# A retention layer followed by a low-rank mixer and an MLP: program order on all engines, batch pairs as nine chunks, q and k transposed by DMA, row tiles and column tiles on the tensor engine

## The chip, the cores and the metric

The kernel runs on one core of one Trainium2 chip. The metric is the device time of the program in microseconds (us), as the median of several runs. Engines: PE is the tensor engine (matmul), PEld its weight loads, DVE the vector engine, ACT the scalar engine, POOL the GpSimd engine, SP an engine that does nothing but issue DMAs in these kernels.

## The reference

There are 8 batches of 576 tokens, 8 heads of 64 dimensions, a mixer of rank 32 over the tokens, and an MLP 512 -> 2048 -> 512. Inputs and outputs are float32; the kernel computes in bfloat16.

```python
scores = (q @ k.T) / 8                       # per batch and head, 576 x 576
D[i, j] = gamma_h ** (i - j) if i >= j else 0
x = (scores * D) @ v                         # heads side by side: 576 x 512 per batch
h = (x.T @ U @ V).T                          # mixes tokens: U is 576 x 32, V is 32 x 576
u = x + h
out = u + relu(u @ w_ch1) @ w_ch2
```

The kernel does not form the 576 x 576 scores. It works in chunks of 128 tokens. The decay is put into factors of the rows of q and v. Within a chunk it computes scores, masks them ("ret") and multiplies by v; what the earlier chunks of the batch give comes from a running state S = sum of k^T v, by q x S.

## The kernel before

576 is four chunks of 128 and one of 64, so a pair of batches is ten chunks, two of them half empty. Each chunk is loaded as float32 from the SP queue, cast on DVE and scaled on POOL, transposed on PE, and evicted (copied out of PSUM, the memory that matmuls write) on ACT. A 64-row matmul stands in the trace as 64*128, a full one as 128*128, and two of them, one for each half of the rows, start together (120.630 and 120.634 us in the trace of the kernel before, the next two 0.067 later):

```python
def T(c):                                    # 8 transposes of q and k on PE, one eviction on ACT
    for j in range(2):
        for hp in range(NHP):
            nc.tensor.transpose(pst[:, j*NHP+hp, :], t[:, j, 2*hp:2*hp+2, :]..., ident)
    nc.scalar.activation(out=qkT, in_=pst, func=AF.Copy)
def SC(c):                                   # scores: 64-row matmuls, one per head; then the mask on DVE
    nc.tensor.matmul(psc[:, hl, hp, 0:n], qkT[pb:pb+HALF, NHP+hp, :], qkT[pb:pb+HALF, hp, cols], ...)
    nc.vector.tensor_tensor(out=rv[...], in0=psc[...], in1=tri[...], op=ALU.mult)
def RV(c):                                   # ret x v, then q x state over all 128 rows
    nc.tensor.matmul(po[:, h*D:(h+1)*D], ret[:, h, :], t[:, 2, h, :], ...)
    nc.tensor.matmul(po[:, hp*P:(hp+1)*P], qkT[:, hp, :], s_sb[:, hp, :], ...)
    ...
for s in range(NC + 2):                      # order of one batch's attention
    if s < NC:          add(T, s, 460)
    if 0 <= s - 2:      add(RV, s - 2, 450)
    if s < NC - 1:      add(ST, s, 220)
    if 0 <= s - 1 < NC: add(SC, s - 1, 450)
```

`q x state` needs the state without its off-diagonal head blocks, so DVE multiplies it by a block mask. `U^T x` is one 128 x 512 matmul per chunk, with U padded from 32 to 128 columns. The attention and mixer of batch b+1 are interleaved with the MLP of batch b; only PE is in program order, and the scheduler orders the other engines:

```python
with tc.manual_schedule(engines={PE}):
    interleave([], front_items(0))
    for b in range(B):
        if b + 2 < B:
            load_batch(b + 2)
        fill = front_items(b + 1) if b + 1 < B else []
        interleave(mlp_items(b, us[b], pairs[b // 2]), fill)
```

Below, "Y1" is the first MLP product (with the relu on ACT as its eviction), "Y2" the second, and "a pair" is two batches, 1152 tokens.

## Time and profile before

| | before |
|---|---|
| time, median | 395.88 us |
| first Y1 starts | 52.84 us |
| one pair in the steady state (first Y1 of batch 2 to that of batch 4) | 87.3 us |
| from the start of the last matmul to the end | 4.3 us |

The page of the kernel before: busy time of the engines (with the share of the span), then busy tenths of PE, the granted clock of PE and the DMA share in 40 equal slices of the span.

```profile
PE 348.4 (88%) x2784; PEld 200.0 (51%) x2784; DVE 183.1 (46%) x249; ACT 156.2 (40%) x279; POOL 64.2 (16%) x83
...
PE   1244489999999999899999999899999999999996
...
PEclk9999959999999999999999999999999999999999
DMA  8999999726995599485149500011001100010012
```

PE is nearly full from the sixth slice on. No other engine is near full there; DMA is, in some slices up to the 22nd. Before the sixth slice DMA is full and PE is not. The busy time by stretch shows the steady state of the kernel before: batch 2's MLP (with batch 3's attention), then batch 3's. Columns: stretch in us and its length, then busy us and number of instructions of each engine, granted clock, DMA share, GB/s.

```profile
core 0: us, PE busy (x) PEld busy (x) DVE busy (x) ACT busy (x) POOL busy (x), PEclk, DMA share, GB/s
141.32:182.00 40.68, 38.73 (x311) 20.35 (x311) 24.14 (x29) 16.84 (x26) 7.29 (x7) 1.00 0.90 182
182.00:228.58 46.58, 45.40 (x388) 27.90 (x386) 25.14 (x30) 21.46 (x43) 5.21 (x5) 1.00 0.47 109
```

PE is idle for 3 us of these 87. The waits of PE in the kernel before, from 95 to 356 us (total us, times, longest; the second line stands there three times, once per pair):

```profile
PE po L270 <- DVE ret L257: 5.8, 9, 1.1
PE ps_y_1610 L390 <- ACT uT_1496 L354: 0.7, 1, 0.7
```

The instructions of PE in order of time show where that wait stands. Columns: start, duration, engine, line, operation, output and inputs, shapes, count, and in brackets the idle time ahead and what ended it. Durations of matmuls overlap, so what a group costs is read from the distance between starts.

```profile
120.63 0.40 PE L246 MATMUL psc<-qkT 64*128 64x128 bf16 x8
120.96 1.04 PE L401 MATMUL ps_y_1358<-w_sb,y_1027 128*128 128x512 bf16 x4
122.35 0.41 PE L270 MATMUL po<-qkv,ret 128*128 128x64 bf16 x8 [0.35 <-DVE ret L257]
122.59 0.39 PE L277 MATMUL po<-s_sb,qkT 128*128 128x128 bf16 x4
```

Scores cost 0.33 us of PE (120.63 to 120.96), q x state 0.23 (from 122.59 to the next MLP matmul at 122.82). Ahead of the scores stands a gap of 0.1 us: they start 0.31 us after the last full matmul, where full ones of 512 columns follow each other at 0.216. Behind them stands another of 0.09: the last two of the eight start at 120.81, the pairs are 0.056 apart, and the next full matmul comes at 120.96. The texts call these gaps a switch. Only one group of MLP matmuls stands between the scores and `ret x v`; the mask takes 1221 ns on DVE, so PE waits. The eight transposes of a chunk cost 0.45 us (61.17 to 61.62):

```profile
61.17 0.61 PE L207 MATMUL pst<-ident,qkv 128*128 128x128 bf16 x8
61.62 1.03 PE L390 MATMUL ps_y_638<-uT_474,w_sb 128*128 128x512 bf16 x4
```

### The profile page before, as it was taken

Reading aid. Unit: us, or ns where it says so; the run is one execution under the profiler, and the core shown is the slowest. Engines: PE = TensorE matmul, PEld = TensorE weight load, DVE = VectorE, ACT = ScalarE, POOL = GpSimd, SP = SyncE. Lnnn points to the kernel's source line nnn. Section 1 sums busy time; section 2 is a strip of 40 time slices with the busy share of each in tenths; the row PEclk is TensorE's granted clock in tenths of the full one; section 3 lists DMA queues with packets and bytes.
Section 4 is the critical chain, followed back from the end, with each engine's and each line's share of the span. In section 5 each row is a group of like instructions: output and inputs, shape, how many; then the busy total and the mean of one; then the engine's idle time right before and its main releaser. Section 6 shows DMA issues by size and latency. Waiting matters only on the chain. (4 is left out here: it accounts for less than half of the span.)

```text
span 394.6 us, 6659 instructions
## 1 busy us (share of the span) xinstructions
PE 348.4 (88%) x2784; PEld 200.0 (51%) x2784; DVE 183.1 (46%) x249; ACT 156.2 (40%) x279; POOL 64.2 (16%) x83
## 2 busy tenths in 40 slices
PE   1244489999999999899999999899999999999996
PEld 0233245446774455446764455346764455456642
DVE  4436326655456555753557445743334533540021
ACT  2121147305770156216760266117750276027700
POOL 6486123301321212210122002200000000000000
PEclk9999959999999999999999999999999999999999
DMA  8999999726995599485149500011001100010012
GB/s 157 217 184 197 198 224 212 131 69 166 223 209 124 150 207 213 98 196 139 25 97 207 140 28 1 28 42 40 2 2 55 55 27 2 28 53 27 2 53 81
DMA packets 123471, 42.49 MB, mean 108 GB/s; under 512 B 114705, under 2 KB 118833, under 8 KB 123441
## 3 DMA queue, kind: packets, MB, share of 16 engines
q1 hardware_dynamic: 117696, 37.76, 43.4%
q0 software_dynamic: 5744, 4.31, 7.2%
q8 instruction: 22, 0.36, 0.4%
q14 instruction: 9, 0.07, 0.1%
HBM read 36.92 MB, written 9.44 MB: 117 GB/s over the span
## 5 line engine op out<-in xcount | busy, mean ns | idle before, releaser
L390 PEld LDWEIGHTS <-w_sb 128*128 128x128 bf16 x768 | 70.4, 98 | 39.1 <-issue 4.7
L185 POOL TENSOR_TENSOR qkv<-stage_t,vscale 128x512 bf16<-128x512 f32 x32 | 34.7, 1085 | 128.3 <-DMA stage_t<-in_v_dram 65.3
L257 DVE TENSOR_TENSOR ret<-psc,tri 128x1024 bf16<-128x1024 f32 x32 | 39.1, 1221 | 9.3 <-PE psc L246 9.1
L328 ACT ACTIVATE a_sb<-psa 128x512 bf16<-128x512 f32 x8 | 4.8, 597 | 97.2 <-PE psa L322 97.2
L184 DVE CAST qkv<-stage_t 128x1024 bf16<-128x1024 f32 x32 | 30.9, 966 | 24.2 <-PE po L270 12.1
L232 DVE TENSOR_TENSOR s_sb<-pss,bdm 128x512 bf16<-128x512 f32 x32 | 22.1, 689 | 41.5 <-PE pss L225 41.5
L216 ACT ACTIVATE qkT<-pst 128x1024 bf16<-128x1024 bf16 x32 | 32.8, 1024 | 20.1 <-PE pst L207 19.1
L287 DVE TENSOR_TENSOR xt<-po,qscale 128x512 bf16<-128x512 f32 x32 | 22.0, 688 | 33.3 <-PE po L277 25.0
L207 PE MATMUL pst<-ident,qkv 128*128 128x128 bf16 x256 | 21.3, 231 | 15.4 <-DVE qkv L184 14.7
L207 PEld LDWEIGHTS <-qkv 128*128 128x128 bf16 x256 | 18.1, 104 | 22.1 <-DVE qkv L184 15.5
L344 DVE TENSOR_TENSOR ut<-ph,xt 128x512 bf16<-128x512 f32 x32 | 22.0, 690 | 11.9 <-PE ph L335 11.7
L270 PE MATMUL po<-qkv,ret 128*128 128x64 bf16 x256 | 13.7, 200 | 8.2 <-DVE ret L257 8.2
L270 PEld LDWEIGHTS <-ret 128*128 128x128 bf16 x256 | 11.6, 102 | 16.9 <-DVE ret L257 13.8
L225 PE MATMUL pss<-qkv 128*128 128x128 bf16 x112 | 11.6, 231 | 6.7 <-POOL qkv L185 6.7
L351 PE MATMUL pu<-ident,ut 128*128 128x128 bf16 x128 | 13.0, 227 | 4.3 <-DVE ut L344 3.8
L351 PEld LDWEIGHTS <-ut 128*128 128x128 bf16 x128 | 10.0, 101 | 12.7 <-DVE ut L344 5.2
L335 PE MATMUL ph<-a_sb,Vbig 128*128 128x512 bf16 x40 | 14.8, 392 | 0.7 <-ACT a_sb L328 0.7
L225 PEld LDWEIGHTS <-qkv 128*128 128x128 bf16 x112 | 9.2, 103 | 11.1 <-issue 6.8
L246 PE MATMUL psc<-qkT 64*128 64x128 bf16 x256 | 13.6, 229 | 0.0
L246 PEld LDWEIGHTS <-qkT 64*128 64x128 bf16 x256 | 7.7, 98 | 11.2 <-issue 11.2
L401 PEld LDWEIGHTS <-y_4127 128*128 128x128 bf16 x80 | 7.8, 98 | 9.3
L277 PE MATMUL po<-s_sb,qkT 128*128 128x128 bf16 x112 | 11.5, 229 | 0.0
(541 smaller groups left out, 615.7 us busy)
## 6 DMA issues: line engine op xcount, KB each, us to landing
out_dram<-o_sb SPq DMA_DIRECT2D x36, 256.0 KB, 2.1
stage_t<-in_k_dram SPq DMA_DIRECT2D x32, 256.0 KB, 4.8
stage_t<-in_q_dram SPq DMA_DIRECT2D x32, 256.0 KB, 4.9
stage_t<-in_v_dram SPq DMA_DIRECT2D x32, 256.0 KB, 5.0
w_sb<-in_moe_w_ch_dram POOLq DMA_DIRECT2D x16, 128.0 KB, 6.7
w_sb<-in_moe_w_ch_dram POOLq DMA_DIRECT2D x8, 256.0 KB, 10.0
stage_t<-in_k_dram SPq DMA_DIRECT2D x8, 128.0 KB, 3.8
stage_t<-in_q_dram SPq DMA_DIRECT2D x8, 128.0 KB, 3.8
```

The costliest lines, as they stand in the source:

```text
L184: nc.vector.tensor_copy(out=t[rows, 0:2, :, :], in_=f[rows, 0:2, :, :])
L185: nc.gpsimd.tensor_tensor(out=t[rows, 2, :, :], in0=f[rows, 2, :, :], in1=vscale[rows, c, :, None].to_broadcast([L, H, D]), op=ALU.mult,)
L207: nc.tensor.transpose(pst[:, j * NHP + hp, :], t[:, j, 2 * hp:2 * hp + 2, :].rearrange("p h d -> p (h d)"), ident,)
L216: nc.scalar.activation(out=qkT, in_=pst, func=AF.Copy)
L232: nc.vector.tensor_tensor(out=s_sb, in0=pss, in1=bdm[:, None, :].to_broadcast([P, NHP, P]), op=ALU.mult,)
L246: nc.tensor.matmul(psc[:, hl, hp, 0:n], qkT[pb:pb + HALF, NHP + hp, :], qkT[pb:pb + HALF, hp, cols], start=True, stop=True,)
L257: nc.vector.tensor_tensor(out=rv[:, :, :, cols], in0=psc[:, :, :, 0:n], in1=tri[:, None, None, cols].to_broadcast([P, 2, NHP, n]), op=ALU. ...
L270: nc.tensor.matmul(po[:, h * D:(h + 1) * D], ret[:, h, :], t[:, 2, h, :], start=(h == 0), stop=True, skip_group_check=True,)
L287: nc.vector.tensor_tensor(out=xt[rows, :].rearrange("p (h d) -> p h d", d=D), in0=po[rows, :].rearrange("p (h d) -> p h d", d=D), in1=qsca ...
L344: nc.vector.tensor_tensor(out=ut[rows, :], in0=ph[rows, :], in1=x_tiles[c][rows, :], op=ALU.add)
L351: nc.tensor.transpose(pu[:, cc, :], u_tiles[c][:, cc * P:(cc + 1) * P], ident)
L390: nc.tensor.matmul(ps[:, 0:n], w1_sb[:, cc, f * P:(f + 1) * P], uT[:, cc, t0:t0 + n], start=(cc == 0), stop=(cc == NCC - 1),)
```

## The change

Its intent: less work on PE, no waits on PE in the steady state, and an earlier first Y1. It has seven parts.

1. All engines run in program order, so the program's own interleaving decides what each engine does next.
2. A pair of batches is nine chunks; the middle one holds the end of one batch and the start of the next, with a mask of its own.
3. q and k are transposed by DMA in pairs 1 to 3 (27 chunks). Pair 0 keeps PE, as the data come late there.
4. q x state is eight 64-row matmuls right behind the scores, which are 64-row matmuls already. Each head uses its own rows, so the state needs no block mask, and ACT copies it.
5. U^T x is five matmuls of 32 columns each, the first four written to four different groups of 32 rows of pa. V is loaded four times to sum the four parts.
6. Scores and mask are one work item, `ret x v` the next, with MLP work in between. Items are spread evenly over the MLP.
7. At the start k and q are loaded ahead of v, and the weights in pieces between. Outputs are issued from POOL, not SP.

```diff
-    with tc.manual_schedule(engines={PE}):
+    with tc.manual_schedule():
 ...
+    def xbar(pr, i):
+        nc.sync.dma_start_transpose(out=c["qkT"], in_=c["qk"].rearrange("p j n -> p (j n)"))
 ...
+        def A(i):
+            SC(pr, i)
+            if i not in (0, J):
+                QS(pr, i)
+            mask(pr, i)
+        def Bf(i):
+            RV(pr, i)
+            if i == J:
+                QS(pr, i)
+            XS(pr, i)
+            if i not in (J, NI - 1):
+                ST(pr, i)
+                Scopy(pr, i)
 ...
+    def QS(pr, i):                            # row tiles: each head's 64 rows
+                r = slice(hl * HALF, (hl + 1) * HALF)
+                nc.tensor.matmul(c["po"][m, hl, hp * D:(hp + 1) * D],
+                    c["qkT"][r, hp, m], s_sb[r, hp, hl * D:(hl + 1) * D], ...)
 ...
+        def MA():                             # column tiles: 32 columns each
+            for n, i in enumerate(idx):
+                g = slice((n % 4) * R, (n % 4 + 1) * R)
+                nc.tensor.matmul(pa[g, :], Ub[:, n, :], st["x", pr][:, i, :],
+                    start=(n < 4), stop=True, skip_group_check=True)
 ...
-                nc.sync.dma_start(out=out_flat[...], in_=o_sb)
+                nc.gpsimd.dma_start(out=out_flat[r0:r0 + P, :], in_=o_sb)
 ...
+        for i in range(J + 1, NI):            # after the first batch's mixer, before its first Y1
+            cast_qk(0, i, "act")
+            scale_v(0, i)
+        for f in range(0, NF, 2):
+            load_w2(f)
+        merge(y1_items(0), attn_items(0, 1, T=True) + mixer_items(0, 1), aux_items(NI, NI + 5))
```

## The prediction

> **What bounds the kernel now.** The tensor engine (PE), after a slow start. The instructions in order of time show the first MLP matmul at 52.8 us, the last at 390.7; the busy-time table shows PE about 97% busy between, at full clock except from 40 to 60 us (0.87, then 0.62). DVE (46%), ACT (40%) and POOL (16%) have room. DMA is saturated only to about 65 us (768 KB of q, k, v per 3.8 us).
>
> Two batches take 87.2 us (first MLP matmul of batch 2, 141.3 us, to that of batch 6, 315.85, halved). Their MLP is 9 chunks of 6.86 us (last batch, alone: 34.3 us for five): 61.7 us. PE work of attention and mixer, from distances between starts: q/k transposes 10 x 0.445, scores 4.1, ret x v 2.35, q x state 1.8, state 1.8, U^T x 10 x 0.216, V 2.2, u transposes 2.0; together 20.8 us. The other 4.7 us are waits and switches; the waits view names ret x v waiting for the mask (1221 ns on DVE), 1.9 us in each even batch, and the first Y1 behind uT, 0.7.
>
> **Steady state, per pair of batches.**
> - q/k transposes leave PE in pairs 1 to 3: -4.45 us.
> - q x state as 64-row tiles beside the scores, which already are such tiles. [...]eight 64-row score matmuls take 0.33 us, eight full transposes of as many columns 0.445, with a 0.1 us gap ahead of the scores. Estimate 0.12 us for 0.226: -0.7.
> - U^T x in four column tiles: two rounds of 0.216 plus switching, for five: -0.8.
> - Nine chunks, not ten: ret x v -0.25.
> Together -6.2 us. Masks move one item (about 2 us) ahead of their use; waits should fall from 4.7 to 2 or 3 us. Estimate 78 to 80 us per pair.
>
> ACT gains q casts and state copies (about 0.6 us each) and loses evictions (1.02); DVE falls; outputs go through POOL. None nears saturation. Transposing DMAs add 27 x 256 KB; DMA was under 10% busy after 230 us, and loads now spread over the run: I expect them hidden.
>
> **Start.** Loading k and q first and w1 in pieces should bring the first Y1 to about 40 us. But ACT, now in program order, must cast q of chunks 5 to 8 before any relu; nine chunks at 3.8 us and w1 (half of the weights' 7.2% of the span, 14 us) put that near 48 us; three PSUM buffers let some three Y1 groups run ahead. w2 and chunks 9 to 11 are DMA-bound until 70 to 75 us. So Y1 of batch 0 with batch 1's front should end near 75 us, against 81 in the same accounting before. Gain 6 us.
>
> **Sum.** 75 + remaining MLP 233 + three pairs' front 43.8 + waits 6 + tail 4.5 = about **362 us**, range **350 to 374**. Faster by over 2%: 0.95; within 2%: 0.04; slower: 0.01.
>
> **Right if** PE is near 97% from 75 us on; no q/k transposes on PE after the second batch; a pair takes 78 to 80 us; ACT waits for loads of q, and PE for ACT, between 40 and 50 us; scores plus q x state take 0.45 us; U^T x under 0.7 us per batch; transposing DMAs land within some us, long before the scores.
>
> **Wrong if** transposing DMAs are slow or block the loads behind them in the SP queue (scores then wait on DMA in pairs 1 to 3, 370 to 385 us); strict order on ACT or DVE makes relu wait behind a late cast; [...]or the start overlaps better than I think (350).

Two terms are estimates. The 0.12 us for q x state is about half of what the scores take without a gap, (0.33 - 0.1) / 2, as it has 64 columns for their 128. The "two rounds of 0.216" for U^T x presume that four column tiles run together, which no trace showed at that time.

## The result, and the profile after

| | before | after |
|---|---|---|
| time, median | 395.88 us | 367.56 us |
| first Y1 starts | 52.84 us | 41.91 us |
| one pair in the steady state | 87.3 us | 76.9 us |
| from the start of the last matmul to the end | 4.3 us | 8.7 us |

The ratio of the times is 0.9285 (95% interval 0.9267 to 0.9302). Ratios are the mean time of one kernel's fast runs over that of the other's fast runs of the same rounds, so they are not quite the ratio of the medians in the table.

The two traces account for the whole difference of their spans, 394.6 - 366.2 = 28.4 us, read from the starts of the first Y1 of batches 2, 6 and 7, of the last matmul, and the end: 7.0 us up to batch 2, 20.7 in the two pairs of batches 2 to 5, 4.8 in batch 6, 0.3 in batch 7, and -4.4 after the last matmul.

The page of the changed kernel, the same lines:

```profile
PE 327.5 (89%) x2600; PEld 181.7 (50%) x2600; DVE 130.0 (36%) x180; ACT 162.3 (44%) x300; POOL 78.5 (21%) x114
...
PE   1466758899999999999999999999999999999990
...
PEclk9999978999999999999999999999999999999996
DMA  9999999997686982597567786786564300110010
```

PE has 21 us less work; DMA has more and spreads over the run; and the last slice of PE is empty, where before it was 6 tenths full. The busy time by stretch of the changed kernel, for batch 2's and batch 3's MLP:

```profile
134.34:169.27 34.93, 34.93 (x272) 17.26 (x271) 14.82 (x19) 16.69 (x28) 6.42 (x8) 1.00 0.59 134
169.27:211.26 41.99, 41.99 (x362) 25.20 (x361) 16.97 (x22) 20.74 (x44) 8.13 (x10) 1.00 0.74 157
```

PE's busy time equals the stretch: by the profile, which models the ends of matmuls, it never stands still. The waits view finds no wait of PE between 78 and 358 us. PE in order of time in the changed kernel:

```profile
213.41 1.90 PE L415 MATMUL ps_y<-uT,w_sb 128*128 128x512 bf16 x8
215.25 0.40 PE L228 MATMUL psc<-qkT 64*128 64x128 bf16 x8
215.48 0.28 PE L253 MATMUL po<-s_sb,qkT 64*128 64x64 bf16 x8
215.69 1.90 PE L415 MATMUL ps_y<-uT,w_sb 128*128 128x512 bf16 x8
217.43 0.40 PE L267 MATMUL po<-vt,ret 128*128 128x64 bf16 x8
```

Scores and q x state together take 0.44 us (215.25 to 215.69) where they took 0.33 and 0.23 apart. Two Y1 groups, 1.7 us, stand between the scores and `ret x v`. The transposing DMAs do their work out of sight. The list of DMA issues has them landing in 3.2 us, against 4.1 to 5.1 for the loads of q, k and v:

```profile
stage_t<-in_k_dram SPq DMA_DIRECT2D x32, 256.0 KB, 4.1
...
stage_t<-in_v_dram SPq DMA_DIRECT2D x32, 256.0 KB, 5.1
...
qkT<-qk SPq DMA_TRANSPOSE x27, 3.2
```

The start still has losses. PE of the changed kernel in the first Y1 groups:

```profile
41.91 1.86 PE L415 MATMUL ps_y<-uT,w_sb 128*128 128x512 bf16 x4 [1.11 <-ACT uT L387]
...
44.25 1.89 PE L415 MATMUL ps_y<-uT,w_sb 128*128 128x512 bf16 x4
45.93 0.95 PE L210 MATMUL pst<-ident,qk 128*128 128x128 bf16 x8
49.30 1.18 PE L415 MATMUL ps_y<-uT,w_sb 128*128 128x512 bf16 x4 [2.42 <-ACT y L420]
```

and ACT at the same time:

```profile
48.13 0.63 ACT L186 ACTIVATE qk<-stage_t 128x512 bf16<-128x512 f32 x1 [2.92 <-DMA stage_t<-in_q_dram]
48.67 0.58 ACT L420 ACTIVATE y<-ps_y 128x512 bf16<-128x512 f32 x1
```

The first relu runs at 48.67 us, right behind the cast of q of the last chunk of the pair, though its matmuls had started at 41.91.

The end of the run, all engines, as the trace has it (start and end in us; this is not an answer of the profile's views):

```
before   391.43 391.76  SP    output DMA issued, landed 393.45
         393.78 393.78  SP    drain
         394.04 394.13  POOL  drain
         394.6          end
after    358.96 359.50  POOL  output DMA issued, landed 361.25
         361.61 361.62  SP    drain
         358.94 365.12  POOL  drain
         366.2          end
```

In the changed kernel POOL's closing drain lasts until 3.9 us after the last output has landed.

### The profile page after: what moved, and what is told of

It is laid out like the page before. It is cut to its first block, busy times and chain, and to the rows that moved or that the text cites. A ratio compares the mean times of both kernels' runs of the same rounds, so it can differ in the third digit from the quotient of the medians.

```text
span 366.2 us, 6281 instructions
## 1 busy us (share of the span) xinstructions
PE 327.5 (89%) x2600; PEld 181.7 (50%) x2600; DVE 130.0 (36%) x180; ACT 162.3 (44%) x300; POOL 78.5 (21%) x114
## 4 chain that ended last, share of the span: by engine, by line
PE 50%; issue 28%; SPq 8%; POOL 5%; DMA 3%; ACT 2%; DVE 2%; POOLq 0%
PE ps_y L436 21%; PE ps_y L415 20%; SPq L174 8%; POOL vt L193 3%; PE psc L228 2%; PE po L267 2%; POOL out_dram L445 2%; DMA stage_t<-in_v_dram 1%; PE pu L383 1%; DMA stage_t<-in_q_dram 1%; DVE ret L238 1%; PE pss L293 1%; PE ph L370 1%; ACT qkT L214 1%; ACT y L420 1%
## 5 line engine op out<-in xcount | busy, mean ns | idle before, releaser
L415 PE MATMUL ps_y<-uT,w_sb 128*128 128x320 bf16 (+1 forms) x768 | 138.1, 330 | 3.5 <-ACT y L420 2.4
L436 PE MATMUL ps_y<-w_sb,y 128*128 128x512 bf16 x576 | 132.0, 379 | 0.0
L420 ACT ACTIVATE y<-ps_y 128x320 bf16<-128x320 f32 (+1 forms) x192 | 93.4, 490 | 53.6 <-PE ps_y L415 43.1
L436 PEld LDWEIGHTS <-y 128*128 128x128 bf16 x576 | 54.0, 98 | 61.9 <-issue 2.5
L445 POOL DMA_DIRECT2D out_dram<-o_sb x36 | 20.3, 564 | 231.3 <-DVE o_sb L442 160.6
L442 DVE TENSOR_TENSOR o_sb<-ps_y,u 128x512 f32<-128x512 f32 x36 | 24.8, 690 | 67.2 <-PE ps_y L436 67.1
L193 POOL TENSOR_TENSOR vt<-stage_t,vscale 128x512 bf16<-128x512 f32 x36 | 37.7, 1056 | 47.2 <-DMA stage_t<-in_v_dram 23.8
L373 DVE TENSOR_TENSOR u<-ph,xt 128x1024 bf16<-128x1024 f32 (+1 forms) x20 | 22.4, 1118 | 32.0 <-PE ph L370 32.0
L186 ACT ACTIVATE qk<-stage_t 128x512 bf16<-128x512 f32 x36 | 22.3, 623 | 10.4 <-DMA stage_t<-in_q_dram 10.4
L301 ACT ACTIVATE s_sb<-pss 128x512 bf16<-128x512 f32 x32 | 19.1, 596 | 17.0 <-PE pss L293 16.0
```

Of the source, the lines that this page charges most:

```text
L193: nc.gpsimd.tensor_tensor(out=c["v"], in0=c["f"][:, 2, :, :], in1=vscale[:, i, :, None].to_broadcast([P, H, D]), op=ALU.mult,)
L373: nc.vector.tensor_tensor(out=st["u", par][:, i0 - base:i0 - base + n, :], in0=ph[:, 0:n, :], in1=st["x", pr][:, i0:i0 + n, :], op=ALU.add,)
L415: nc.tensor.matmul(ps[:, 0:n], w1_sb[:, cc, f * P:(f + 1) * P], st["uT", par][:, cc, t0:t0 + n], start=(cc == 0), stop=(cc == NCC - 1),)
L420: nc.scalar.activation(out=st["y1", par][:, f, t0:t0 + n], in_=ps[:, 0:n], func=AF.Relu)
L436: nc.tensor.matmul(ps, st["y1", par][:, f, c * P:(c + 1) * P], w2_sb[:, f, :], start=(f == 0), stop=(f == NF - 1),)
L442: nc.vector.tensor_tensor(out=o_sb, in0=ps, in1=st["u", par][:, c, :], op=ALU.add)
```

## The experiments

Twelve kernels ran. All gave correct results. They came in three sets, each beside its own runs of the kernel before, whose medians were 396.62, 395.99 and 395.94 us; so times of different sets, which ran on different chips, can be compared to within about 0.7 us. The changed kernel's own time is 367.56 us. Every edit is to the changed kernel but in the last one.

### e1_tail_sp: the last outputs from SP

```diff
-                nc.gpsimd.dma_start(out=out_flat[r0:r0 + P, :], in_=o_sb)
+                out_eng = nc.sync if (pr == B // 2 - 1 and par == 1) else nc.gpsimd
+                out_eng.dma_start(out=out_flat[r0:r0 + P, :], in_=o_sb)
```

> The changed kernel with the five outputs of the last batch issued from the SP queue instead of POOL. Theory A: the end of the kernel (8.3 us after the last matmul, for 3.9 us before the change) is held by POOL's closing drain, which lasts until about 5.6 us after its last DMA issue although the data had landed 3.9 us earlier; with POOL long idle at the end the tail should be about 4 us and the time 363.3 us (-4.2). Rival B: the tail is only the longer landing of an output sent through POOL (2.8 for 2.1 us) and its longer issue: then -1 us, 366.6.

Measured: 362.24 us, ratio to before 0.9131. In the trace the time from the start of the last matmul to the end fell from 8.7 to 4.1 us. The last output was issued at 357.94 and landed at 359.94; POOL's drain took 0.1 us (360.28 to 360.38); the end came at 360.86. Theory A holds: it was POOL's drain, not the transfer.

### e2_late_casts: the casts of chunks 6 to 8 behind the first relus

```diff
-        for i in range(J + 1, NI):
-            cast_qk(0, i, "act")
-            scale_v(0, i)
+        cast_qk(0, J + 1, "act")
+        for i in range(J + 1, NI):
+            scale_v(0, i)
 ...
+            if T and i + 1 < NI:
+                items.append(lambda i=i: (A(i), cast_qk(pr, i + 1, "act")))
 ...
```

> The changed kernel with the casts of q and k of chunks 6, 7 and 8 moved from ahead of the first Y1 into the work of the chunk before, so that no relu stands behind them on ACT. Theory A: PE's loss between 42 and 57 us comes from relus that stand behind the cast of q of chunk 8 (done at 48.7 us); first relu near 44 us, and 4 us less in all, 363.6. Rival B: the stretch is bound by the loads[...] and the wait only moves: less than 1 us.

Measured: 361.87 us, ratio 0.9122, so 5.7 us less, and theory A holds in kind. The first relu ran at 42.51 us. The gain is more than the 4 us of the forecast. The busy time by stretch, from the first Y1 to the end of the stretch with gaps, shows why. First the changed kernel:

```profile
41.90:77.50 35.60, 27.89 (x232) 14.11 (x232) 12.82 (x16) 19.70 (x32) 13.04 (x15) 0.90 1.23 211
```

Then this run:

```profile
40.60:71.20 30.60, 25.66 (x231) 12.85 (x231) 13.81 (x17) 19.69 (x32) 11.79 (x14) 1.00 1.14 202
```

The same PE instructions are busy 2.2 us less, at a mean granted clock of 1.00 in place of 0.90. The clock record in the trace of the changed kernel has full clock from 46.6 to 50.0 us, then half from 50.0 to 56.9, right after PE had stood still for 2.4 us; in this run it is full from 45.8 us on. (Both records begin there; the groups of four Y1 matmuls before it took 1.86 us for the later 1.03, so PE was at half speed then too.) So two losses go with the late relu: the wait, and the half clock right behind it. That the wait brought the clock down is the estimate from these traces; what sets the clock was not shown. (The trace of e1, whose start is that of the changed kernel, has no full clock before 57.3 us: there PE was at half speed before and after the wait, and the stretch from the first Y1 to the first Y2 is as long, 56.7 us for 56.5.) The pieces of the record of the changed kernel in this stretch are 3.41 us (full) and 6.83 us (half). DMA's share is still 1.14 in this stretch, so rival B is right only in that a bound by loads exists; it did not bind first.

### e8_tail_and_casts: both

> Both of the two edits above. If A holds for both and they add up: about 359.4 us; if only the tail: 363.

Measured: 357.87 us, ratio 0.9018 (0.8984 to 0.9052). The two gains nearly add up (5.3 and 5.7 us alone, 9.7 together). This kernel is the fastest.

### e3_pe_transposes: q and k transposed on PE again

```diff
-            if pr > 0:
-                xbar(pr, i)
 ...
-            if T:
+            if True:
                 items.append(lambda i=i: pe_T(pr, i))
```

> The changed kernel with q and k of pairs 1 to 3 transposed on PE again (eight transposes and an ACT eviction per chunk), no transposing DMA. Theory A: PE is without a gap from 77 us on, so what is put back costs its full PE time, 27 x 0.445 = 12.0 us: 379.6 us, a pair 80.9 us in place of 76.9. Rival B: the transposing DMAs or their place in the SP queue cost something of their own: clearly less than 12. Rival C: the eviction and one more hop bring new waits: clearly more than 12.

Measured: 389.43 us, 21.9 us more, and a pair takes 84.4 and 84.9 us. Theory A is too small and rival B is out. The waits of PE in this run, from 80 to 385 us, name the new wait:

```profile
PE po L267 <- DVE ret L238: 3.6, 12, 0.5
```

`ret x v` waits for the mask again. With three items per chunk instead of two, each item is followed by less MLP work. This view counts only the matmuls' idle time; PE's weight loads of the same line were idle for longer (from 130 to 310 us 8.0 us in 12 waits, the matmuls 2.4 us in 8). So it is rival C, but not by the hop it named: the edit had also changed the spacing. The next run keeps the spacing.

### e12_transposes_grouped: the same, with the spacing kept

Each chunk's eight transposes sit in the item of the chunk before, so a chunk has two items as in the changed kernel.

```diff
+            if T or i in (J, NI - 1):
                 items.append(lambda i=i: Bf(i))
+            else:
+                items.append(lambda i=i: (Bf(i), pe_T(pr, i + 1)))
```

> As e3 (q and k of pairs 1 to 3 transposed on PE), but each chunk's transposes sit in the work item of the chunk before, so that the number of items, and with it the MLP work between scores and ret x v, is that of the changed kernel. e3 took 84.6 us per pair where the added PE work explains 80.9. Theory A: the other 3.7 us came from the denser items, which left the mask less to hide behind: now 80.9 to 81.5 us per pair, no wait of ret x v for the mask, 379 to 381 us in all. Rival B: the PE transposes bring the waits themselves, through ACT's evictions and PSUM: 84 us per pair and 388 us again.

Measured: 381.84 us; a pair takes 82.3 and 82.0 us. The waits view finds no wait of PE from 80 to 385 us. So of the 7.7 us per pair that e3 lost, 4.0 is the work itself (9 x 0.445), 2.5 is the spacing (e3 less this run), and 1.2 stays as small gaps that the weight loads show ("issue", up to 0.4 us each) and that no run took apart. Both figures lie just above theory A's (80.9 to 81.5 and 379 to 381 us), so it holds in the main; the transposes by DMA are worth 5.2 us per pair.

### e4_qs_apart: q x state away from the scores

```diff
         def A(i):
             SC(pr, i)
-            if i not in (0, J):
-                QS(pr, i)
             mask(pr, i)
         def Bf(i):
+            if i not in (0, J):
+                QS(pr, i)
             RV(pr, i)
```

> The changed kernel with q x state still as 64-row tiles, but issued ahead of ret x v (one item later) instead of right behind the scores. Theory A: the gain lies in sharing one stay in the 64-row mode; alone, the block pays the switch in and out again, about 0.2 us in place of nothing, for 24 blocks in all: +5 us, about 372.5, and the block takes about 0.33 us by distances between starts for 0.12 beside the scores. Rival B: only the two parallel tiles matter: within 1 us of 367.6.

Measured: 371.59 us, 4.0 us more; a pair takes 78.4 us, 1.5 more, which is 0.21 us for each of the seven blocks that moved. PE in order of time:

```profile
216.21 0.40 PE L228 MATMUL psc<-qkT 64*128 64x128 bf16 x8
216.54 1.90 PE L415 MATMUL ps_y<-uT,w_sb 128*128 128x512 bf16 x7
218.38 0.29 PE L253 MATMUL po<-s_sb,qkT 64*128 64x64 bf16 x8
218.60 0.41 PE L267 MATMUL po<-vt,ret 128*128 128x64 bf16 x8
```

(one of the eight Y1 matmuls is missing from the trace). Eight at 0.216 us end at 218.27, so the block takes 0.33 us up to 218.60: 0.11 of gap and 0.22, where beside the scores it adds 0.11 to their 0.33. Theory A holds: a second block of 64-row matmuls among full ones costs 0.21 us, about the two gaps of 0.1 and 0.09 us that stand ahead of and behind the scores in the kernel before. What PE does in these gaps was not shown.

### e5_u_full: U^T x in full-width matmuls

U is padded with zeros to 128 columns and V is loaded once.

```diff
-                g = slice((n % 4) * R, (n % 4 + 1) * R)
-                nc.tensor.matmul(pa[g, :], Ub[:, n, :], st["x", pr][:, i, :],
-                    start=(n < 4), stop=True, skip_group_check=True)
+                nc.tensor.matmul(pa, Ub[:, n, :], st["x", pr][:, i, :],
+                    start=(n == 0), stop=(n == len(idx) - 1))
 ...
-        for g in range(4):
+        for g in range(1):
             nc.gpsimd.dma_start(out=V4[g * R:(g + 1) * R, HALF:HALF + S], in_=moe_V)
```

> The changed kernel with U^T x as five full-width matmuls of 128 x 512 per batch (U padded with zeros, as before the change), not in four column tiles. Theory A: five at 0.216 us, 1.08 us, for about 0.6 us in column tiles with its switch: +0.45 us per batch, +3.6 us in all, about 371. Rival B: the column tiles lose as much[...] as they win: within 1 us.

Measured: 366.37 us, 1.2 us less, although a pair takes 77.8 us, 0.9 more, just as theory A has it. PE of the changed kernel shows the block in column tiles:

```profile
156.81 0.60 PE L346 MATMUL pa<-xt,U_O 128*32 128x512 bf16 x5
157.35 0.82 PE L436 MATMUL ps_y<-w_sb,y 128*128 128x512 bf16 x3
```

Five matmuls take 0.54 us, with 0.09 of gap ahead (the two Y2 matmuls before them start at 156.29 and so end at 156.72), where five full ones at 0.216 us take 1.08. So the steady state is as expected and the time is not: the stretch up to the first Y2 was 3.5 us shorter (94.85 for 98.38 us). The next run asks why.

### e11_u_full_four_v: the same, with four loads of V

> As e5 (U^T x in full-width matmuls), but with V still loaded four times, as in the changed kernel; e5 loaded it once. e5 took 77.8 us per pair, 0.88 more than the changed kernel, as forecast, yet ended 1.2 us earlier, because its stretch before the first Y2 was 2.8 to 3.5 us shorter. Theory A: that came from the three V loads that were not made (loads and casts a little earlier, so that PE's idle gap at 46 us stayed short and its clock stayed up): with four loads the first Y2 is near 97.5 us again, and the time 369 to 371 us. Rival B: it came from the full-width matmuls themselves ahead of the first Y1: first Y2 near 95 us, and 366.4 us again. Either way a pair takes 77.8 us.

Measured: 368.74 us, a pair in 77.8 us, the first Y2 at 96.63 us. The total is just below what theory A had, and only half of its mechanism holds. The first relu ran at 46.35 us here and at 46.42 in e5, so the loads did not come later. But PE had started its first Y1 0.9 us earlier (40.30 for 41.17 us; why is not known), so its gap before that relu was longer, 1.86 us for 1.37. And the clock record differs: full from 44.9 us on in e5, half from 48.1 to 55.0 in e11. The pieces of the record are multiples of 3.41 us (in the traces of the kernel before and of the changed kernel 3.41, 6.83 and 10.24 us up to the long full piece). Cut into steps of that length, it has the gap in one step; the busy times there, e5 first, then e11:

```profile
44.93:48.34 3.41, 1.77 (x14) 0.78 (x11) 0.18 (x1) 2.46 (x5) 1.20 (x2) 1.00 1.36 218
44.72:48.13 3.41, 1.42 (x11) 0.57 (x8) 0.34 (x1) 2.32 (x5) 1.05 (x2) 1.00 1.32 219
```

In the changed kernel the same step (46.6 to 50.0 us) has PE busy for 0.99 us, in e2 (45.8 to 49.2) for 2.08; in the kernel before, the step at full clock ahead of its half clock (44.0 to 47.4) has 1.17. So of these five steps half clock came after those with 0.99, 1.17 and 1.42 us of PE work, and full clock after those with 1.77 and 2.08. That PE's work in that one step decides it is the estimate from these five; that the three further loads of V brought it about is not shown. With four loads in both, column tiles are worth 1.2 us in all (368.74 for 367.56), little more than the 0.7 us to which sets compare, and the 95% intervals of the two ratios overlap (0.9281 to 0.9334 for 0.9267 to 0.9302). The steady state shows 0.44 us per batch, 3.5 in eight; the start gives back most of it, and part of that is chance: the first Y1 is at 41.91 us in the trace of the changed kernel, but between 40.8 and 41.2 in e1, e3, e4, e6 and e12, which share its start.

### e6_mask_close: no MLP work between scores and ret x v

```diff
-            items.append(lambda i=i: A(i))
-            items.append(lambda i=i: Bf(i))
+            items.append(lambda: None)
+            items.append(lambda i=i: (A(i), Bf(i)))
```

> The changed kernel with scores, mask and ret x v of a chunk in one work item, so that no MLP matmuls stand between the scores and ret x v. Theory A (the waits of the steady state are gone because the mask gets 2 us of MLP work to hide behind): each of 31 chunks makes PE wait 1.2 us for the mask[...]: +40 us or more, about 410. Rival B (the waits are gone for another reason, the order on the other engines): under +10 us.

Measured: 403.53 us, 36.0 us more and slower than the kernel before (ratio 1.0182, 95% interval 1.0161 to 1.0204). A pair takes 88.6 us. The waits of PE from 80 us on:

```profile
PE po L267 <- DVE ret L238: 33.8, 27, 1.6
```

27 waits of 1.25 us, about the length of the mask (1.22). (Theory A's 40 us held a term per chunk; 31 waits of 1.2 us alone come to 37.) Theory A holds in kind, a little under its 40 us: this spacing alone decides whether the whole change gains or loses.

### e7_pe_order_only: program order on PE alone

```diff
-    with tc.manual_schedule():
+    with tc.manual_schedule(engines={mybir.EngineType.PE}):
```

> The changed kernel with program order only on PE, as before the change; the other engines are ordered by the scheduler. Theory A: with the work spaced as it is, the order on DVE, ACT, POOL and SP does not matter in the steady state: pairs stay within 0.5 us of 76.9, and only the start moves (within 5 us of 367.6). Rival B: program order on all engines is what removed the waits of the steady state: a pair is again 2 to 4 us longer, 375 to 380 us.

Measured: 378.23 us, 10.7 us more. Pairs take 77.2 and 76.9 us, so theory A holds for the steady state and rival B falls. But the start moved by 13 us, to 54.92 us, and not within the 5 us that A allowed. The waits of the run's first 40 us:

```profile
PE pst L210 <- ACT qk L186: 27.0, 5, 10.6
ACT qk L186 <- DMA stage_t<-in_q_dram: 21.4, 5, 9.4
POOL vt L193 <- DMA stage_t<-in_v_dram: 11.0, 1, 11.0
```

Everything waits for the loads of q and v. With POOL free to run ahead, it issued w1 and part of w2 by 22.6 us, and the first v was scaled at 33.6 us in place of 21.2. That these weights took the DMA from q and v is a reading of this trace, which the next run tests.

### e10_pe_pool_order: program order on PE and POOL

> As e7 (program order on PE only), but with program order on PE and on POOL. In e7 the weights were issued from POOL without waiting for v, and v of the first chunk came at 33 us in place of 20; the first Y1 moved from 41 to 55 us. Theory A: it is POOL's program order alone that holds the weights back behind v, so this run starts like the changed kernel: first Y1 within 2 us of 41 us, time within 3 us of 367.6. Rival B: the order on ACT, DVE or SP matters as well: first Y1 clearly later than 43 us.

Measured: 374.62 us. The first Y1 is at 42.60 us, so theory A holds for it: POOL's order is what holds the weights back. But the time is 7.1 us above the changed kernel, outside A's 3. The order on the other engines matters as well, though not for the first Y1, where rival B had looked for it. In the trace 4.4 us of it stand before the first Y2 (102.79 for 98.38 us), and 2.2 in two pairs of the steady state (78.6 and 77.5 us), where a wait of 1.1 us for the mask came back; so e7's finding, that the order does not matter there, does not hold for every such order. DVE in this run, before the first Y2:

```profile
68.28 0.43 DVE L184 CAST qk<-stage_t 128x512 bf16<-128x512 f32 x1 [6.27 <-DMA stage_t<-in_k_dram]
68.62 1.22 DVE L238 TENSOR_TENSOR ret<-psc,tri 128x1024 bf16<-128x1024 f32 x1
```

and PE:

```profile
65.28 0.40 PE L228 MATMUL psc<-qkT 64*128 64x128 bf16 x8 [1.60 <-ACT qkT L214]
65.51 0.28 PE L253 MATMUL po<-s_sb,qkT 64*128 64x64 bf16 x8
...
69.89 0.61 PE L267 MATMUL po<-vt,ret 128*128 128x64 bf16 x8 [3.13 <-DVE ret L238]
```

The scheduler had put a cast of k of a later chunk ahead of the mask. The scores were ready at 65.5 us, but DVE stood waiting for the load until 68.28, and PE waited 3.1 us for the mask. The clock record then has half clock from 68.1 to 78.3 us.

### b1_rv_later: the kernel before, with ret x v one stage later

```diff
-        for s in range(NC + 2):
+        for s in range(NC + 3):
 ...
-            if 0 <= s - 2:
-                add(RV, s - 2, 450)
+            if 0 <= s - 3:
+                add(RV, s - 3, 450)
```

and four buffers instead of three for qkT, ret and the state.

> The kernel before the change with one edit: ret x v of a chunk is issued one stage later (behind the scores of two chunks later), with one more buffer of each kind that lives longer. Theory A: the 4.7 us per pair that were neither MLP nor counted work were mostly ret x v waiting for the mask, in the last two chunks of each batch, where no transposes stand between: a pair falls from 87.2 to about 84.5 us, and the time from 395.9 to about 388. Rival B: they are switches between array modes and other gaps: less than 1 us per pair, 393 to 396.

Measured: 389.98 us, 6.0 us less than the kernel before, ratio 0.9844. Pairs take 86.2 and 84.9 us, 1.7 us less on average. No wait for the mask is left; the waits of PE between 95 and 356 us are now

```profile
PE ps_y L390 <- ACT uT L354: 2.1, 3, 0.7
PE po L270 <- DVE xt L287: 1.2, 1, 1.2
```

So the mask was a real wait of the kernel before, but only about 1.7 of the 4.7 us per pair that the prediction called waits and switches; theory A was right in kind and too large. The busy time by stretch shows 3.1 us per pair as idle PE in the kernel before: the mask, 0.7 us for uT once per pair, and small gaps. The other 1.6 us do not show as idle time; no run took them apart.

## Why the prediction was right or wrong

It said 362 us, with a range of 350 to 374; measured, 367.56. What bounds the kernel was right: PE in the steady state, loads at the start. The terms:

- **Steady state, "78 to 80 us per pair": 76.9.** The work taken off PE was sized well: scores with q x state 0.44 us for a forecast of 0.45, and U^T x -0.9 us for -0.8 (e5). The transposes are worth 5.2 us (e12: nine chunks, with small gaps) for 4.45 (ten chunks). The term that was off is "waits should fall from 4.7 to 2 or 3 us": by the prediction's own sum they fell to 0.6 us (76.9 less 61.7 of MLP and 20.8 - 6.2 of other work), and the waits view has none. e6 shows that the spacing holds them off: without MLP work between, 27 waits of 1.25 us come back. b1 shows that the mask's wait had been only 1.7 of the 4.7 us; what else fell away was not taken apart.
- **Start, "near 75 us" for Y1 of batch 0 with the front of batch 1: 77.5**, where the gapless stretch begins. The mechanism was as said: the first Y1 at 41.9 (forecast 40), and ACT held by the cast of q of chunk 8 until 48.7 (forecast 48). e2 shows it by taking it away. Not foreseen: that PE's clock would stand at half for 6.8 us right after the gap (50.0 to 56.9 us).
- **"Tail 4.5": 8.3** (from the last matmul's modelled end; 8.7 from its start). This was the term most in error. The forecast does not say what its 4.5 us hold; the trace shows POOL's closing drain, and e1 takes 4.6 us off by ending on SP.
- **Transposing DMAs hidden: right.** They land in 3.2 us, and one wait for them appears, of a weight load and 0.3 us long. The loads that run beside them land in 4.1 to 5.1 us, but those come from DRAM, so this does not compare the two kinds of DMA.
- **Together.** 75 + 282.8 + 4.5 = 362.3 was forecast; 77.5 + 280.4 + 8.3 = 366.2 is the span of the trace (the execution that was traced took 367.99 us, 1.8 above its span). That two misses of about 2.5 us cancel is luck; the tail's is what remains. Two parts of the change had no run of their own: the nine chunks, and loading k and q ahead of v.

"Strict order on ACT or DVE makes relu wait behind a late cast" was named as a danger, and was counted in the start. That strict order also *gives* 10.7 us (e7) was not forecast: 3.6 of them come with POOL's order, which keeps the weights behind the first loads, and 7.1 with the order on the other engines (e10).

## What to carry to other kernels

When PE is the bound, put enough of its other work between a product and the use of what another engine makes of it: 1.7 us for a mask of 1.2 here, and check that an edit does not change the spacing as well as the work. Program order on a queue that issues DMAs worked here as a priority for the transfers (with it on POOL the first Y1 came at 42.60 us, without it at 54.92; e10, e7), and program order on an engine that also casts loaded data let one late load stop everything behind it (the first relu at 48.67 us, and at 42.51 with the casts later; e2); so place such casts as late as their use allows. Look at the end of the trace as closely as at the middle: five DMAs issued from another queue were worth 5 us.
